# Linear attention and MLP-mixer on one core: the last batch's products pair by pair, its outputs on other queues, single load buffers from batch 4 on

## The chip, the cores and the metric

The kernel runs on one core of one Trainium2 chip. The metric is the device time of one execution in microseconds (us). The profile's span is some 1.8 us shorter than the device time (262.1 against 263.9 for the profiled run of before); it runs from the first instruction to the end of the last.

## The reference

```python
# q, k, v: [8 batches, 8 heads, 576, 64]
phi = lambda x: np.where(x > 0, x, np.exp(x) - 1.0) + 1.0
kv  = einsum('bhsd,bhse->bhde', phi(k), v);  z = phi(k).sum(axis=2)
x   = einsum('bhsd,bhde->bhse', phi(q), kv) / (einsum('bhsd,bhd->bhs', phi(q), z)[..., None] + 1e-6)
x   = x.transpose(0, 2, 1, 3).reshape(8, 576, 512)
u   = x + (relu(x.T @ w_tok1) @ w_tok2).T        # token mixing, per batch
out = u + relu(u @ w_ch1) @ w_ch2                # channel mixing, 512 -> 1536 -> 512
```

## The kernel before

Batches are taken one after the other. While TensorE (PE) does the channel mixing of batch n, the attention and token mixing of batch n + 1 and the preparation of batch n + 2 are put in between its matmuls at fixed steps. The order on every engine is the order of the program; no scheduler changes it.

576 rows are four row tiles of 128 and a rest of 64. The rests ("tails") of two batches share one tile, which is done with the odd batch. In batches 6 and 7 the last matrix product of the four row tiles is not done tile by tile. Two row tiles (pair j, 0 or 1) and two halves of the columns make a 2 by 2 block matrix, which is multiplied with seven products in place of eight (Strassen's scheme). Each product is six matmuls of 256 columns. Products 1, 6, 7 and 4 add up in one PSUM tile, X (where the matmuls leave their sums), which VectorE (DVE) must read between them:

```python
def product(n, j, i):          # i: which of the seven, j: which pair of row tiles
    lhs, rhs, tile_, first = {1: (..., "X", True),  2: (..., "Z", True), 6: (..., "X", False),
                              5: (..., "Y", True),  7: (..., "X", False), 4: (..., "X", False),
                              3: (..., "Y", False)}[i]
    ...                        # six matmuls into the PSUM tile, then DVE adds it to o
    if i in (4, 3):            # a row tile is complete: two transfers of 128 KB
        d, r = (1 if i == 4 else 0), 2 * j + (1 if i == 4 else 0)
        for e in range(2):
            nc.gpsimd.dma_start(out=outv[n, :, 2 * r + e], in_=o[half[e], d])

ORDER = [(1, 0), (1, 1), (2, 0), (6, 0), (2, 1), (6, 1), (5, 0), (7, 0), (5, 1), (7, 1),
         (4, 0), (3, 0), (4, 1), (3, 1)]
```

The very last work is the shared tail tile, in a part of 384 and one of 128 columns, whose outputs go out on SP's and ScalarE's (ACT's) queues:

```python
def mm4_last(cs):
    ...                        # 12 matmuls, one DVE addition
    for b in range(2):
        (nc.scalar if b else nc.sync).dma_start(out=outv[2 * p + b, :, 2 * R, cs], in_=o[half[b]])
...
big = m3(n) + m3t + m4s(n) + [                                   # batch 7
    lambda: mm4_last(slice(0, DM - 128)), lambda: mm4_last(slice(DM - 128, DM))]
```

Operands that the seven products need are sums of weight blocks (GpSimd, once) and of activation blocks ("row sums", DVE, in each of the two batches). They are kept in load buffers that are no longer used.

## Time and profile before

| | before |
|---|---|
| device time, median of 3 runs (263.83 with the fourth, which the comparison below has) | 263.8 us (263.64 to 263.93) |
| span of the profile | 262.1 us |
| PE busy | 249.9 us |
| start of PE's last matmul | 254.97 us |
| from there to the end of the span | 7.16 us |

The chain of waits that ended last, in order of time; the columns are start in us, us, and what. These are its last pieces:

```profile
249.30 0.67 PE h_ps L605 x6
...
251.50 0.45 POOL out_dram L629
...
254.09 1.04 POOL out_dram L629 x2
255.13 0.52 POOLq L895
```

The reader is to see that the chain leaves PE at 249.97 and runs to the end through GpSimd (POOL): through its eight output issues and then through "POOLq L895", GpSimd's sequencer at the kernel's closing line. It says that GpSimd stood at the end of what the program waited for last. The chain stops at 255.65 although the span ends at 262.1, so it doesn't say what GpSimd did in the rest.

### The profile page before, as it was taken

How to read it: one execution, taken by the hardware profiler on the slowest of the kernel's cores; microseconds unless marked ns; L12 is line 12 of the kernel's file. 1: busy time of each engine (PE TensorE's matmuls, PEld its weight loads, DVE VectorE, ACT ScalarE, POOL GpSimd, SP SyncE). 2: the span in 40 equal slices, each digit the busy share in tenths (PEclk: the TensorE clock that was granted, in tenths of full speed). 3: DMA queues.
4: the chain of work that ended last, by engine and by line, in shares of the span. 5: the costliest groups of instructions: out<-in, count | busy, mean ns of one | idle time of the engine just before them, and what ended most of it. 6: DMA issues, size and time to landing. Idle time of an engine off the chain costs nothing.

```text
span 262.1 us, 5249 instructions
## 1 busy us (share of the span) xinstructions
PE 249.9 (95%) x2142; PEld 138.4 (53%) x2142; DVE 161.9 (62%) x317; ACT 131.2 (50%) x205; POOL 65.6 (25%) x92
## 2 busy tenths in 40 slices
PE   7799999999999999999999999999999999999990
PEld 3574465646644544455644544455644545756970
DVE  5875859865966376837652575838862486815550
ACT  4755853387580569146670569046670543046100
POOL 9850300110011100110003100179909500060060
PEclk9999999999999999999999999999999999999996
DMA  7999999799049951899999972660083403350033
GB/s 254 254 204 293 351 232 399 243 265 407 9 114 198 393 210 25 179 258 406 409 253 172 373 277 42 149 164 0 16 156 81 123 0 23 80 160 3 0 100 103
DMA packets 49576, 48.35 MB, mean 184 GB/s; under 512 B 30288, under 2 KB 35536, under 8 KB 49552
## 3 DMA queue, kind: packets, MB, share of 16 engines
q1 hardware_dynamic: 41184, 34.35, 43.6%
q0 software_dynamic: 8208, 13.54, 23.3%
q8 instruction: 17, 0.28, 0.5%
q10 hardware_dynamic: 160, 0.13, 0.2%
q14 instruction: 7, 0.06, 0.1%
HBM read 35.85 MB, written 9.44 MB: 173 GB/s over the span
## 4 chain that ended last, share of the span: by engine, by line
PE 79%; DMA 10%; POOL 3%; DVE 2%; issue 1%; ACT 1%; POOLq 0%; DVEq 0%
PE c_ps L480 28%; PE h_ps L506 26%; DMA wc<-in_moe_w_ch_dram 7%; PE a_ps L246 6%; PE c_ps L494 4%; PE h_ps L259 4%; PE nd_ps L208 3%; PE h_ps L605 3%; DMA cr<-in_v_dram 3%; PE kv_ps L167 2%; PE y_ps L605 1%; POOL out_dram L629 1%; DVE o_sb L611 1%; POOL qT L673 1%; DVE ut L284 1%
## 5 line engine op out<-in xcount | busy, mean ns | idle before, releaser
L487 ACT ACTIVATE cr<-c_ps 128x512 bf16<-128x512 f32 x91 | 53.5, 599 | 77.2 <-PE c_ps L480 77.1
L480 PE MATMUL c_ps<-uT,wc 128*128 128x512 bf16 x384 | 91.4, 379 | 0.1
L506 PE MATMUL h_ps<-wc,cr 128*128 128x512 bf16 x288 | 66.0, 379 | 0.4 <-DMA wc<-in_moe_w_ch_dram 0.4
L480 PEld LDWEIGHTS <-wc 128*128 128x128 bf16 x384 | 35.7, 98 | 36.7 <-issue 1.7
L528 POOL DMA_DIRECT2D out_dram<-o_sb x24 | 14.5, 608 | 130.8 <-DVE o_sb L523 130.6
L506 PEld LDWEIGHTS <-cr 128*128 128x128 bf16 x288 | 27.4, 98 | 32.2 <-DMA wc<-in_moe_w_ch_dram 0.9
L220 DVE TENSOR_TENSOR x<-nd_ps,den 128x512 bf16<-128x512 f32 (+1 forms) x42 | 25.3, 602 | 1.5
L523 DVE TENSOR_TENSOR o_sb<-h_ps,u 128x512 f32<-128x512 f32 x24 | 16.4, 689 | 13.2 <-PE h_ps L506 13.0
L124 ACT ACTIVATE e<-q_raw 128x1152 bf16<-128x1152 f32 x16 | 18.5, 1160 | 5.6 <-DMA q_raw<-in_q_dram 5.4
L138 DVE TENSOR_TENSOR qp<-e,y 128x1152 bf16<-128x1152 bf16 x16 | 12.3, 770 | 12.3 <-ACT e L124 11.8
L124 ACT ACTIVATE e<-k_raw 128x1152 bf16<-128x1152 f32 x16 | 18.7, 1169 | 2.4 <-DMA k_raw<-in_k_dram 2.4
L217 DVE TENSOR_SCALAR den<-nd_ps 128x8 f32<-128x8 f32 (+1 forms) x42 | 6.9, 163 | 19.9 <-PE nd_ps L208 19.2
L271 DVE TENSOR_TENSOR u<-h_ps,x 128x1024 bf16<-128x1024 f32 x12 | 14.7, 1222 | 6.2 <-PE h_ps L259 6.2
L629 POOL DMA_DIRECT2D out_dram<-o_sb x16 | 8.3, 527 | 40.4 <-DVE o_sb L611 40.4
L138 DVE TENSOR_TENSOR kp<-e,y 128x1152 bf16<-128x1152 bf16 x16 | 12.1, 757 | 8.0 <-ACT e L124 7.4
L208 PEld LDWEIGHTS <-qT 128*128 128x128 bf16 x140 | 11.4, 98 | 9.3 <-issue 0.2
L208 PE MATMUL nd_ps<-kvbd,qT 128*128 128x130 bf16 x140 | 15.1, 223 | 0.0
L246 PE MATMUL a_ps<-x,w 128*128 128x512 bf16 x56 | 14.4, 379 | 0.0
L130 DVE TENSOR_SCALAR y<-q_raw 128x1152 bf16<-128x1152 f32 x16 | 13.6, 849 | 0.9 <-DMA q_raw<-in_q_dram 0.9
L149 ACT CAST vs<-v_raw 128x1152 bf16<-128x1152 f32 x12 | 13.9, 1160 | 0.0
L130 DVE TENSOR_SCALAR y<-k_raw 128x1152 bf16<-128x1152 f32 x16 | 12.0, 753 | 1.4 <-DMA k_raw<-in_k_dram 1.3
L259 PE MATMUL h_ps<-ar,w2p 128*128 128x512 bf16 x48 | 12.3, 379 | 0.0
(120 smaller groups left out, 282.9 us busy)
## 6 DMA issues: line engine op xcount, KB each, us to landing
k_raw<-in_k_dram SPq DMA_DIRECT2D x16, 576.0 KB, 9.8
q_raw<-in_q_dram SPq DMA_DIRECT2D x16, 576.0 KB, 7.1
v_raw<-in_v_dram SPq DMA_DIRECT2D x14, 576.0 KB, 11.1
out_dram<-o_sb POOLq DMA_DIRECT2D x24, 256.0 KB, 5.0
wc<-in_moe_w_ch_dram POOLq DMA_DIRECT2D x8, 384.0 KB, 9.3
out_dram<-o_sb POOLq DMA_DIRECT2D x22, 128.0 KB, 3.4
cr<-in_v_dram POOLq DMA_DIRECT2D x2, 288.0 KB, 6.9
w<-in_moe_w_tok_dram POOLq DMA_DIRECT2D x1, 288.0 KB, 7.2
```

What stands on the lines that cost most here:

```text
L124: nc.scalar.activation(out=e, in_=f, func=AF.Exp)
L130: nc.vector.tensor_scalar(out=y, in0=f, scalar1=1.0, scalar2=1.0, op0=ALU.add, op1=ALU.max)
L138: nc.vector.tensor_tensor(out=dst.transpose([0, 2, 1, 3]), in0=e.rearrange("p (i t d) -> p i t d", i=nj, t=T), in1=y.rearrange("p (i t d) ...
L208: nc.tensor.matmul(out=o[:, a], lhsT=qT[b][:, t0:t0 + 128], rhs=kvbd[b][:, c, a], start=True, stop=True)
L220: nc.vector.tensor_tensor(out=x[b][:, rs[0]:rs[0] + m, HG * D * g:HG * D * (g + 1)].rearrange("p r (h d) -> p r h d", h=HG), in0=v_[:, :, ...
L246: nc.tensor.matmul(out=ps[:, mt], lhsT=w1t[:, b, ms] if r == R else w1[:, r, ms], rhs=x[b][:, r, :], start=(r == 0), stop=(r == R))
L259: nc.tensor.matmul(out=ps[:, i], lhsT=w2v(kt, r, b), rhs=ar[b][:, kt, :], start=(kt == 0), stop=(kt == NT - 1 and not add))
L271: nc.vector.tensor_tensor(out=u[b][:, rs[0]:rs[0] + m], in0=ps[:, 0:m], in1=x[b][:, rs[0]:rs[0] + m], op=ALU.add)
L480: nc.tensor.matmul(out=ps, lhsT=wc1[:, kj, 128 * mc:128 * mc + 128], rhs=uT[b][:, :, kj], start=(kj == 0), stop=(kj == NDM - 1))
L487: nc.scalar.activation(out=cr[b][:, mc, :], in_=ps, func=AF.Relu)
L506: nc.tensor.matmul(out=ps, lhsT=crt[:, kc, :] if t == 8 else cr[b][:, kc, 128 * r:128 * r + 128], rhs=wc2[:, kc, :], start=(kc == 0), stop ...
L523: nc.vector.tensor_tensor(out=o, in0=ps, in1=u[b][:, r, :], op=ALU.add)
```

## The change

Its intent: the last batch's first pair of row tiles is completed, and sent out, long before the end; GpSimd issues none of the last batch's outputs; the tail tile fills a wait between two products. From batch 4 on each tensor has one load buffer instead of two, with loads about one batch ahead, which frees buffers so that the weight sums can start early in batch 5. The tails' token mixing is moved behind batch 6's products. (The diff is cut; where the operands' buffers are renamed it only follows from this.)

```diff
+    def rb(n):
+        return n % 2 if n < 4 else 0
-        return after(nc.sync.dma_start(out=raw[nm, n % 2][:, js], in_=src_[:, js]), gate)
+        return after(nc.sync.dma_start(out=raw[nm, rb(n)][:, js], in_=src_[:, js]), gate)
 ...
-    def mm4_last(cs):            # (removed)
 ...
-        if i in (4, 3):
-            d, r = (1 if i == 4 else 0), 2 * j + (1 if i == 4 else 0)
+        queues = [nc.sync, nc.scalar] if n + 1 == B else [nc.gpsimd] * 2
+        if n + 1 == B and j == 1 and i in (2, 4, 3):
+            d, cs = {2: (0, HC[0]), 4: (1, ALL), 3: (0, HC[1])}[i]
             for e in range(2):
-                nc.gpsimd.dma_start(out=outv[n, :, 2 * r + e], in_=o[half[e], d])
+                queues[e].dma_start(out=outv[n, :, 2 * (2 * j + d) + e, cs], in_=o[half[e], d, cs])
+        elif i == 3:
+            for e in range(2):
+                queues[e].dma_start(out=outv[n, :, 4 * j + e:4 * j + e + 3:2], in_=o[half[e]])
 ...
+    LAST = [(1, 0), (2, 0), (6, 0), (5, 0), (7, 0), (1, 1), (4, 0), (3, 0),
+            (2, 1), (6, 1), (5, 1), (7, 1), None, (4, 1), (3, 1)]     # None: the tail tile
 ...
-                big = m3(n) + m3t + m4s(n) + [
-                    lambda: mm4_last(slice(0, DM - 128)), lambda: mm4_last(slice(DM - 128, DM))]
+            big = m3(n) + m3t + (m4(p, [4, 5, 6, 7, 8]) if n < FIRST else
+                                 m4s(n) + m4(p, [8]) if n + 1 < B else m4s(n, LAST))
 ...
+            if n >= FIRST:
+                at_.update(mm2t=25, utt=25)
 ...
-            fill += [(18, lambda: load_all(n + 4, "qkv"))]
-        if n + 3 == B:
-            fill += [(18 + i, lambda i=i: weight_sums(2 * i, 2)) for i in range(3)]
+            fill += [(k_[1] + 2, lambda: load_all(n + 3, "qkv"))]
+        if n + 1 == FIRST:
+            fill += [(4 * i, lambda i=i: weight_sums(2 * i, 2)) for i in range(3)]
```

More of the change, by code (lines that the diff above doesn't have):

```diff
@@ L121, in phi_exp @@
     def phi_exp(nm, n, j0, nj):
-        f = raw[nm, n % 2][:, j0:j0 + nj].rearrange("p j f -> p (j f)")
+        f = raw[nm, rb(n)][:, j0:j0 + nj].rearrange("p j f -> p (j f)")
         e = work.tile([128, 2 * TD], BF16, name="e", tag="e", bufs=4)[:, :nj * TD]
@@ L127, in phi_add @@
     def phi_add(nm, n, j0, nj):
-        f = raw[nm, n % 2][:, j0:j0 + nj].rearrange("p j f -> p (j f)")
+        f = raw[nm, rb(n)][:, j0:j0 + nj].rearrange("p j f -> p (j f)")
         y = work.tile([128, 2 * TD], BF16, name="y", tag="y")[:, :nj * TD]
@@ L149, in vcast @@
         copy(out=vs[:, js, :, 0:D],
-             in_=raw["v", n % 2][:, js].rearrange("p j (t d) -> p j t d", t=T))
+             in_=raw["v", rb(n)][:, js].rearrange("p j (t d) -> p j t d", t=T))
     def bank():
@@ L535, in mm4_end @@
                 put.dma_start(out=outv[2 * p + b, :, 2 * R], in_=o[half[b]])
-    def mm4_last(cs):
-        p = B // 2 - 1
-        m = cs.stop - cs.start
-        ps = ps_big.tile([128, 512], FP32, name="h2_ps", tag="big")[:, 0:m]
-        for kc in range(NCH):
-            nc.tensor.matmul(out=ps, lhsT=crt[:, kc, :],
-                             rhs=wc2[:, kc, cs], start=(kc == 0), stop=(kc == NCH - 1))
-        o = outp.tile([128, 2, DM], FP32, name="o_sb", tag="o_sb")[:, 0, 0:m]
-        nc.vector.tensor_tensor(out=o, in0=ps, in1=ut[p % 2][:, cs], op=ALU.add)
-        for b in range(2):
-            (nc.scalar if b else nc.sync).dma_start(out=outv[2 * p + b, :, 2 * R, cs],
-                                                    in_=o[half[b]])
     KH = NCH // 2
@@ L557, in bf @@
         return t[:, 1536 * i:1536 * (i + 1)]
-    tb = [bf("k", 0, i).rearrange("p (k c) -> p k c", k=KH) for i in range(3)] + [
-        bf("q", 0, 0).rearrange("p (k c) -> p k c", k=KH)]
-    tf = raw["q", 0].rearrange("p j f -> p (j f)")[:, 768:2304].rearrange("p (k c) -> p k c", k=KH)
-    sb = [(bf("v", 0, i) if i < 3 else bf("v", 1, 0)).rearrange("p (k j s) -> p k j s", k=KH, j=2)
+    FIRST = 6
+    tb = [bf("k", 1, i).rearrange("p (k c) -> p k c", k=KH) for i in range(3)] + [
+        bf("q", 1, 0).rearrange("p (k c) -> p k c", k=KH)]
+    tf = raw["q", 1].rearrange("p j f -> p (j f)")[:, 768:2304].rearrange("p (k c) -> p k c", k=KH)
+    sb = [(bf("v", 1, i) if i < 3 else bf("q", 1, 1)).rearrange("p (k j s) -> p k j s", k=KH, j=2)
           for i in range(4)]
@@ L625, in product, with m4s @@
             add(0, 1, ps, o[:, 0, HC[1]])
-        if i in (4, 3):
-            d, r = (1 if i == 4 else 0), 2 * j + (1 if i == 4 else 0)
+        queues = [nc.sync, nc.scalar] if n + 1 == B else [nc.gpsimd] * 2
+        if n + 1 == B and j == 1 and i in (2, 4, 3):
+            d, cs = {2: (0, HC[0]), 4: (1, ALL), 3: (0, HC[1])}[i]
             for e in range(2):
-                nc.gpsimd.dma_start(out=outv[n, :, 2 * r + e], in_=o[half[e], d])
+                queues[e].dma_start(out=outv[n, :, 2 * (2 * j + d) + e, cs], in_=o[half[e], d, cs])
+        elif i == 3:
+            for e in range(2):
+                queues[e].dma_start(out=outv[n, :, 4 * j + e:4 * j + e + 3:2], in_=o[half[e]])
     ORDER = [(1, 0), (1, 1), (2, 0), (6, 0), (2, 1), (6, 1), (5, 0), (7, 0), (5, 1), (7, 1),
              (4, 0), (3, 0), (4, 1), (3, 1)]
-    def m4s(n):
-        return [lambda i=i, j=j: product(n, j, i) for i, j in ORDER]
+    LAST = [(1, 0), (2, 0), (6, 0), (5, 0), (7, 0), (1, 1), (4, 0), (3, 0),
+            (2, 1), (6, 1), (5, 1), (7, 1), None, (4, 1), (3, 1)]
+    def m4s(n, order=ORDER):
+        out_ = []
+        for e in order:
+            out_ += [lambda e=e: product(n, e[1], e[0])] if e else m4(n // 2, [8])
+        return out_
     def prep_k(n, g, copy=nc.scalar.copy):
@@ L846 @@
         if b == 0:
-            big = m3(n) + (m4s(n) if n + 2 == B else m4(p, [0, 1, 2, 3]))
+            big = m3(n) + (m4s(n) if n >= FIRST else m4(p, [0, 1, 2, 3]))
         else:
-            big = m3(n) + m3t + m4(p, [4, 5, 6, 7, 8])
-            if n + 1 == B:
-                big = m3(n) + m3t + m4s(n) + [
-                    lambda: mm4_last(slice(0, DM - 128)), lambda: mm4_last(slice(DM - 128, DM))]
+            big = m3(n) + m3t + (m4(p, [4, 5, 6, 7, 8]) if n < FIRST else
+                                 m4s(n) + m4(p, [8]) if n + 1 < B else m4s(n, LAST))
         fill = []
         if n + 1 < B:
-            fill += [((AT3 if n == 2 else AT)[nm], fn) for nm, fn in steps(n + 1)]
+            at_ = dict(AT3 if n == 2 else AT)
+            if n >= FIRST:
+                at_.update(mm2t=25, utt=25)
+            fill += [(at_[nm], fn) for nm, fn in steps(n + 1)]
         if n + 2 < B:
@@ L859 @@
             fill += [(12 + d, lambda: qtr_dma(n + 2))]
-            if n == 2:
-                fill += [(16, lambda: load_all(5, "qkv"))]
-            fill += [(s + d, lambda g=g: prep_k(n + 2, g)) for g, s in ((0, 14), (1, 16))]
-            fill += [(18, lambda: load_all(n + 4, "qkv"))]
-        if n + 3 == B:
-            fill += [(18 + i, lambda i=i: weight_sums(2 * i, 2)) for i in range(3)]
-        if n + 2 >= B:
+            k_ = ((14, 16) if n < FIRST else (18, 20) if b == 0 else (14, 21))
+            fill += [(s + d, lambda g=g: prep_k(n + 2, g)) for g, s in enumerate(k_)]
+            fill += [(k_[1] + 2, lambda: load_all(n + 3, "qkv"))]
+        if n + 1 == FIRST:
+            fill += [(4 * i, lambda i=i: weight_sums(2 * i, 2)) for i in range(3)]
+        if n >= FIRST:
             fill += [(9, lambda n=n: row_sums(n, 3, 0, KH))]
```

## The prediction

> **What bounds the kernel now.** I read the page first, then PE's own waits, then the timeline of the last two batches, then the transfers. The page:
>
> ```profile
> PE 249.9 (95%) x2142; PEld 138.4 (53%) x2142; DVE 161.9 (62%) x317; ACT 131.2 (50%) x205; POOL 65.6 (25%) x92
> ...
> PE   7799999999999999999999999999999999999990
> ```
>
> PE (TensorE) is busy in every slice but the first and the last. What PE waits for is therefore the whole budget between them. These are the longest:
>
> ```profile
> PE bank L653 <- DVE ones L666: 1.5, 1, 1.5
> PE bank L178 <- DVE qp L138: 1.3, 1, 1.3
> PE h_ps L605 <- DVE o_sb L611: 0.5, 1, 0.5
> ```
>
> The first two lie in the first 9 us, which the change doesn't touch. No load from batch 1 on makes PE wait. The third lies in batch 6's products (L605: the seven-product scheme that stands in for the last matrix product in batches 6 and 7). Its timeline, cut to that stretch:
>
> ```profile
> 221.47 0.62 PE L280 MATMUL h_ps<-ar,w2p 128*64 128x512 bf16 x4
> 222.03 1.08 PE L605 MATMUL h_ps<-k_raw,v_raw 128*128 128x256 bf16 x6
> ...
> 224.26 0.82 PE L605 MATMUL y_ps<-k_raw,v_raw 128*128 128x256 bf16 x6
> 225.62 0.82 PE L605 MATMUL h_ps<-k_raw,v_raw 128*128 128x256 bf16 x6 [0.54 <-DVE o_sb L611]
> ```
>
> Products start 0.655 us apart when nothing is late (226.27, 226.93, 227.58). So 222.03 to 222.95 holds 0.27 us of waiting (for a row sum that DVE ends at 222.56), and 224.26 to 225.62 holds 0.70: DVE spent 223.73 to 225.11 on the tail's two additions (L284, 0.69 each) and read the accumulator of product 6 only afterwards. The end of the run:
>
> ```profile
> 251.50 4.15 POOL L629 DMA_DIRECT2D out_dram<-o_sb  x8 [18.06 <-DVE o_sb L611]
> ...
> 252.41 2.78 PE L543 MATMUL h_ps<-wc,crt 128*128 128x384 bf16 x24
> ...
> 254.56 0.96 DVE L546 TENSOR_TENSOR o_sb<-h_ps,ut 128x384 f32<-128x384 f32 x2 [1.52 <-PE h_ps L543]
> 255.15 1.19 SPq L548 DMA_DIRECT2D out_dram<-o_sb  x2
> 255.15 1.46 ACTq L548 DMA_DIRECT2D out_dram<-o_sb  x2
> ```
>
> PE issues its last matmul at about 255.03 (call the end of issue T; the row adds 0.16 us of modelled drain, the difference between a 0.82 row and its 0.655 spacing). GpSimd takes 4.15 us to issue eight 128 KB outputs, the last at 255.13. SP and ACT issue four small ones, the last on ACT at about 255.83, landing 3.8 us later by the transfer view: 259.6, or T + 4.6. From there to 262.1 is a close of about 2.5 us.
>
> **What the Trainium skill says.** "DMA: Bandwidth & Descriptors", section "Issuing engines are not separate DMA queues": transfers from all engines run on the same 16 DMA engines, and issuing from several saves only issue time. The trace agrees: DMA is still moving some 240 GB/s from 253 to 258 whoever issued it. The same page, "Anatomy of one DMA", puts most of a transfer's roughly 2 us fixed cost into the write receipt; here outputs of 32 to 128 KB take 2.9 to 4.1 us from issue to landing, little of it size. "SBUF — State Buffer", in its terms, calls the port pair that VectorE and GpSimd share an exclusive lock for a whole instruction. The trace agrees for the q addition that runs beside GpSimd's subtractions: 1.72 us against 0.75 alone, while the subtraction takes 1.67 against 1.16.
>
> **The change part by part.**
>
> *Buffers.* Loads for batches 5, 6 and 7 go to one set of buffers, about a batch before use rather than nearly two. Before, twelve loads were issued from 110.2 to 124.7 and six from 139.5 to 145.9. Now six go after each of three batches' preparation. Batch 5's q is still issued near 110.2 (the SP queue reaches it after the transpose there) and first read at 122.64. Batch 7's follow the tails' transpose, 166.95 + 1.41 = 168.4, and are first read by DVE at 181.16. The median q landing between 130 and 165, with crowded queues, was 6.7 us. Both have 12 us. k and v follow later and have their readers from 131.8 and 189.8. Effect on PE: 0.
>
> *Weight sums.* 18 GpSimd subtractions at 1.16 us start after the same output issues near 173.7 and run through, to about 195 to 197, where six of them ran from 197.85 to 204.6 before. They now overlap batch 7's k additions on DVE (189.8 and 192.8, 0.75 us each, to become perhaps 1.7). DVE was idle 1.90 us waiting for PE soon after, and four PSUM banks of 2.6 us work each stand between its output additions and PE. Effect: 0.
>
> *Tail of batches 6 and 7 moved behind batch 6's last product.* DVE loses 1.38 us in the critical stretch, so the second wait (0.70) goes. But L280 leaves the place where it filled time: product 6 would start at 221.38, run three matmuls (0.33) to 221.71, then wait for the row sum until 222.61. That is 0.90 of waiting in place of 0.27, and the four matmuls (some 0.56) are run later. Sum of the waits: 0.99 + 0.09 of switching before, 0.90 + 0.09 after, so -0.1 us. The transposes after it start near 232; their reader starts at 240.5.
>
> *Last batch's order.* Products of one row pair now follow each other: 1, 2, 6, 5, 7. Product 6 may overwrite nothing before DVE has read product 1, and only one product (0.655) lies between. DVE starts 0.20 after the product's issue ends and takes 0.425, and PE restarts 0.055 after DVE (225.565 to 225.62 above): 0.68 against 0.655, 0.03 us lost. It happens at four places (1 to 6, 6 to 7, 7 to 4, and 6 to 7 of the second pair): +0.1 us. Before, two products lay between.
>
> *Tail tile undivided.* 12 matmuls of 512 columns in place of 12 of 384 and 12 of 128: the same columns; twelve of 512 show 2.75 at 200.59 against 2.78. 0.0.
>
> *Outputs.* The first pair's 512 KB leave at T - 5.9 and are out of the way. GpSimd's eight issues vanish for this batch. But DVE now does the tail (0.69) at T - 1.11, product 4 to T, and product 3 from T + 0.20 to T + 0.62. SP, at 0.55 us an issue plus 0.05 between, has two for the tail from T - 0.37, one for product 4 at T + 0.83 and the last at T + 1.43; ACT starts its last at T + 0.7. Last issue T + 1.43 against T + 0.80 before, 0.63 later. About 640 KB is written in those last microseconds, less than the 1.25 MB of before, so I estimate 3.3 us to landing rather than 3.8, chosen between the 2.9 and 3.8 seen: T + 4.7 against T + 4.6, +0.1 us.
>
> Sum: 0 + 0 - 0.1 + 0.1 + 0.0 + 0.1 = +0.1, so 263.8 becomes 263.9 us.
>
> **Rivals.** First: the end is shorter than I think. For it: GpSimd was issuing until 255.65, and if its queue holds the close open, or if SP and ACT land in 2.9 us without its traffic, 0.3 to 0.6 us are gained: 263.3. Against: the last landing by my reckoning was ACT's, not GpSimd's. Second: SP's row of three issues and the burst behind it give 3.8 us to landing or more, and PE's four restarts lose 0.1 to 0.2 rather than 0.03: +0.6 to +0.9, 264.5. For it: SP really is in order. Third: a load comes too late in its single buffer, as its issue now waits for the previous batch's casts: PE would stand for a microsecond or more, 265. Against: the 12 us of lead. Fourth: GpSimd's lock delays DVE so that PE misses a PSUM bank, up to 1 us, against which stand the four banks.
>
> **Range and chances.** All terms are tenths of microseconds in a span that PE fills; 2% would be 5.3 us, ten times any of them. The spread of the runs of before is 0.3 us. Rival one gives the lower end and rival two the upper: 263.2 to 264.6. Chances: faster by over 2% 0.01, within 2% 0.97, slower by over 2% 0.02.
>
> **What would show it.** Batch 6: no wait of PE on DVE's output addition between products 5 and 7, a wait near 0.9 us inside product 6, and L280's successor behind the last product. Batch 7: four gaps of 0.03 us. Batches 3 to 5: no wait of DVE or ACT on a load. DVE's k addition near 190 longer than 1 us. End: two tail issues before SP's last two, the last SP issue 1.4 us after T, nothing from GpSimd. I would be wrong if ACT or DVE waits on a load of batches 5 to 7, if the close after the last landing isn't 2.5 us, or if batch 6's stretch from 218.55 to 230.20 (11.65 us) isn't 11.5 to 11.6 after.

## The result, and the profile after

The changed kernel took 262.0 us (median of four runs, 261.91 to 262.42) against 263.83 of before (263.64 to 263.93). The ratio is 0.9935, with a 95% interval of 0.9918 to 0.9952. Ratios here are the mean time of one kernel's runs over that of the other's of the same rounds, so not quite the ratio of the medians. The forecast that the time stays within 2% held, but 262.0 lies 1.2 us below the range, and the predicted sign was wrong.

PE's waits of the kernel after, longest first (total us, times, longest); only the third concerns the change:

```profile
PE bank L653 <- DVE ones L666: 1.5, 1, 1.5
PE bank L181 <- DVE qp L141: 1.2, 1, 1.2
PE h_ps L595 <- DVE v_raw L577: 0.7, 1, 0.7
```

Batch 6's products in the timeline of after (start, us, engine, line, operation, shapes, count; in brackets the idle time before, and what ended it):

```profile
221.31 0.49 PE L595 MATMUL h_ps<-k_raw,v_raw 128*128 128x256 bf16 x3
...
222.54 0.50 PE L595 MATMUL h_ps<-k_raw,v_raw 128*128 128x256 bf16 x3 [0.74 <-DVE v_raw L577]
...
224.84 0.82 PE L595 MATMUL h_ps<-k_raw,v_raw 128*128 128x256 bf16 x6
...
229.52 0.62 PE L283 MATMUL h_ps<-ar,w2p 128*64 128x512 bf16 x4
```

The wait before product 7 is gone (224.84 follows 224.19 by one product), product 6 now stands still in its middle, and the tails' four matmuls are at the end. That is what the prediction drew. Now the end of the run, from the timeline of after, with the same columns:

```profile
253.66 0.82 PE L595 MATMUL h_ps<-q_raw,cr 128*128 128x256 bf16 x6
254.31 0.82 PE L595 MATMUL y_ps<-wc,q_raw 128*128 128x256 bf16 x6
254.58 1.11 SPq L538 DMA_DIRECT2D out_dram<-o_sb  x2
255.17 0.42 DVE L601 TENSOR_TENSOR o_sb<-y_ps,o_sb 128x256 f32<-128x256 f32 x1 [0.23 <-PE y_ps L595]
255.78 1.37 SPq L620 DMA_DIRECT2D out_dram<-o_sb  x2
```

PE's last matmul starts at 254.86, 0.11 earlier than before, and SP's row of issues ends at 257.15, later than the 256.34 of before. Yet the span ends at 260.2 instead of 262.1. So the gain is not on PE. The table divides each span by the first of batch n's channel-mixing matmuls (us):

| stretch | before | after |
|---|---|---|
| start, batches 0 and 1 (to the first of batch 2) | 84.93 | 84.85 |
| batch 2 | 27.25 | 27.26 |
| batch 3 | 31.87 | 31.87 |
| batch 4 | 27.25 | 27.26 |
| batch 5 | 31.87 | 31.87 |
| batch 6 | 27.02 | 26.97 |
| batch 7, to the start of the last matmul | 24.77 | 24.78 |
| last matmul to the end of the span | 7.16 | 5.32 |

Of 1.96 us, 1.84 are in the last line. The windows view of that stretch has the columns window, length, busy time of five engines, granted clock, DMA share and GB/s. Before:

```profile
258.50:259.00 0.50, 0.00 (x0) 0.00 (x0) 0.00 (x0) 0.00 (x0) 0.00 (x0) 0.50 0.23 69
259.00:259.50 0.50, 0.00 (x0) 0.00 (x0) 0.00 (x0) 0.00 (x0) 0.00 (x0) 0.50 0.00 0
```

After:

```profile
258.00:258.50 0.50, 0.00 (x0) 0.00 (x0) 0.00 (x0) 0.00 (x0) 0.00 (x0) 0.61 0.88 312
258.50:259.00 0.50, 0.00 (x0) 0.00 (x0) 0.00 (x0) 0.00 (x0) 0.00 (x0) 0.50 0.00 0
```

The last byte moves less than half a microsecond earlier; what follows the last byte shrinks from over 3 us to under 2. The page and the timeline leave out what sequencers do, so I read their records in the trace. A DRAIN is an instruction of an engine's sequencer; these stand at the kernel's closing line (L895), ahead of a closing barrier, at which every engine has to have arrived before the program goes on. These are the rows that decide, put in my words (start us, us, engine, operation; first before, then after):

```
before  254.77  6.58  POOL  DRAIN              until 261.35
        259.62  0.03  SP    wait for the last transfer to land (ACT's, landed 259.61)
        260.00  0.01  SP    arrives at the closing barrier
        261.39  0.02  POOL  finds all arrived, releases the barrier

after   230.77  7.35  POOL  DRAIN              until 238.12
        258.96  0.03  SP    wait for the last transfer to land (SP's, landed 258.94)
        259.40  0.01  SP    arrives at the closing barrier
        259.43  0.02  POOL  finds all arrived, releases the barrier
```

Before, everything had landed and SP was at the barrier at 260.00, but GpSimd, which releases the barrier, was inside a DRAIN until 261.35. After, its DRAIN was over at 238.12, and the barrier followed SP by 0.03. With the same 0.03, the barrier of before would have been at 260.03, so the DRAIN cost 1.36 us. ACT shows no such thing: its DRAIN in before ended at 257.06, 2.55 us before its own last transfer landed, and it is SP that waits, one semaphore after another, for the transfers of all queues.

The other 0.60 of the 1.96 are SP's earlier arrival: 0.11 from PE, 0.56 because the last landing comes 4.08 us after the last matmul's start rather than 4.64, less 0.07 because SP's chain of waits after it is that much longer. The chain view of after no longer has GpSimd at its end; this is its last piece:

```profile
255.17 0.42 DVE o_sb L601
```

### The profile page after: what moved, and what is told of

The parts are those of the page before. It is cut to its first block, busy times and chain, and to the rows that moved or that the text cites. A ratio compares the mean times of both kernels' runs of the same rounds, so it can differ in the third digit from the quotient of the medians.

```text
span 260.2 us, 5195 instructions
## 1 busy us (share of the span) xinstructions
PE 249.1 (96%) x2113; PEld 137.7 (53%) x2130; DVE 164.1 (63%) x316; ACT 130.8 (50%) x205; POOL 61.9 (24%) x80
## 4 chain that ended last, share of the span: by engine, by line
PE 81%; DMA 8%; ACT 3%; POOL 3%; DVE 2%; issue 1%; SPq 0%; POOLq 0%; DVEq 0%; ACTq 0%
PE c_ps L483 28%; PE h_ps L509 26%; PE a_ps L249 5%; PE h_ps L595 4%; PE c_ps L497 4%; DMA k_raw<-in_k_dram 4%; DMA wc<-in_moe_w_ch_dram 4%; PE h_ps L262 4%; PE nd_ps L211 3%; PE y_ps L595 2%; PE kv_ps L170 2%; ACT e L127 1%; POOL qT L673 1%; POOL cr L119 1%; PE h_ps L283 1%
## 5 line engine op out<-in xcount | busy, mean ns | idle before, releaser
L531 POOL DMA_DIRECT2D out_dram<-o_sb x24 | 14.5, 608 | 125.0 <-DVE o_sb L526 124.8
L141 DVE TENSOR_TENSOR kp<-e,y 128x1152 bf16<-128x1152 bf16 x16 | 12.9, 805 | 6.7 <-ACT e L127 6.0
L133 DVE TENSOR_SCALAR y<-k_raw 128x1152 bf16<-128x1152 f32 x16 | 13.7, 856 | 2.9 <-DMA k_raw<-in_k_dram 2.8
L497 PE MATMUL c_ps<-uTt,wc 128*128 128x128 bf16 x192 | 12.0, 219 | 0.0
```

The lines of the kernel that those rows point to most:

```text
L133: nc.vector.tensor_scalar(out=y, in0=f, scalar1=1.0, scalar2=1.0, op0=ALU.add, op1=ALU.max)
L141: nc.vector.tensor_tensor(out=dst.transpose([0, 2, 1, 3]), in0=e.rearrange("p (i t d) -> p i t d", i=nj, t=T), in1=y.rearrange("p (i t d) ...
L497: nc.tensor.matmul(out=ps[:, m], lhsT=wc1[:, kj, 128 * mc:128 * mc + 128], rhs=uTt[:, kj, :], start=(kj == 0), stop=(kj == NDM - 1))
```

## The experiments

Theory D: GpSimd's DRAIN at the close lasts until some 2 us after GpSimd's own last transfer has landed (form 1), or 6.6 to 7.4 us from its own start as in the two traces (form 2), and it held the end. Theory O: the gain comes from the new order of the last batch (the first pair out early, fewer bytes at the end). Theory B: it comes from the buffers, weight sums or tails. All twelve runs gave the correct result. Four calls were made, each on one chip with its own runs of before (medians 263.87, 263.8, 264.01 and 263.88).

### The queues alone

`e1_before_hw_queues` is the kernel before with this edit:

```diff
-                nc.gpsimd.dma_start(out=outv[n, :, 2 * r + e], in_=o[half[e], d])
+                put = nc.gpsimd if n + 1 < B else nc.scalar if e else nc.sync
+                put.dma_start(out=outv[n, :, 2 * r + e], in_=o[half[e], d])
```

> The kernel before, with one edit: the sixteen... that is eight output transfers of batch 7's products that GpSimd issued go half to SP's and half to ACT's queue; order, tails and buffers stay as before. Theory D (GpSimd's closing drain, which ended 2.5 us after the last landing of GpSimd's own transfers, held the end of the program for 1.36 us, and the GpSimd traffic delayed the others' landings): the drain ends early, the last landing comes near 258.5 to 258.9, and the time is 261.6 to 262.1, nearly the whole gain of the change. Theory O (the gain is the order of the last batch: first pair out early, fewer bytes at the end): nothing or a few tenths, 263.4 to 263.9. Theory B (buffers or tails): 263.8.

Measured: 261.43 us (ratio 0.9909, 0.9896 to 0.9922). The DRAIN ended at 237.99, and from the last matmul to the end it took 4.69 us. The time lies 0.17 below what theory D expected. The queues alone bring the whole gain, and a little more than the change. Theory B falls, and O as the main cause.

### The queues undone

`e2_after_gpsimd` is the changed kernel with `queues = [nc.gpsimd] * 2` for every batch.

> The changed kernel with one part undone: batch 7's product outputs go back to GpSimd, in the new order and grouping; the tails' tile stays on SP. Theory D: GpSimd's last issue starts near 256.6, lands about 3 us later, the drain ends 2.0 to 2.5 us after that and the time is 263.8 to 264.8, above even the kernel before, since the new order gives GpSimd its last pieces later. Theory O: near 262.0, at most 262.6. Theory B: 262.0.

Measured: 264.62 us (1.0029, 1.0017 to 1.0041), 0.3% slower than before. GpSimd's last transfer landed at 259.23, its DRAIN lasted until 262.08 (2.85 later, where 2.0 to 2.5 were expected), and the barrier was released at 262.12 although SP was there at 259.70. The new order without the new queues is a loss, as GpSimd then has its last pieces later.

### One transfer on GpSimd

`e3_one_gpsimd` is the changed kernel with one half of the last product's output on GpSimd:

```diff
-                queues[e].dma_start(out=outv[n, :, 2 * (2 * j + d) + e, cs], in_=o[half[e], d, cs])
+                put = nc.gpsimd if i == 3 and e else queues[e]
+                put.dma_start(out=outv[n, :, 2 * (2 * j + d) + e, cs], in_=o[half[e], d, cs])
```

> The changed kernel with a single 64 KB transfer, half of the very last product's output, moved from ACT to GpSimd. Theory D, form 1 (the drain ends 2.0 to 2.5 us after the last landing of GpSimd's transfers): the transfer is issued near 255.65, lands near 258.5, the drain ends near 260.7 and the time is 263.0 to 263.6. Theory D, form 2 (the drain lasts 6.6 to 7.4 us from its own start, as in both traces): drain from about 255.7 to 262.6, time 264.9 to 265.3. Theories O and B: 262.0.

Measured: 263.44 us (0.9993, 0.9976 to 1.001): a single 64 KB transfer gives back most of the gain. The timeline of this run, GpSimd alone:

```profile
257.29 0.54 POOL L621 DMA_DIRECT2D out_dram<-o_sb  x1 [24.34 <-DVE o_sb L601]
```

(The profiled execution was one of the slower ones of this kernel, 264.63, and everything in it from batch 1 on stands 1.4 us later.) The transfer landed at 259.99 and the DRAIN ran from 257.27 to 262.08, 4.81 us. So the DRAIN has no fixed length, and form 2 falls. It ended 2.09 after the landing, as form 1 has it, and the barrier was released 1.19 after SP's arrival.

### Early transfers on GpSimd

`e4_early_gpsimd` is the changed kernel with `nc.gpsimd` for the first pair's two transfers.

> The changed kernel with only the first row pair's outputs of batch 7 (512 KB in two transfers, issued near 249.1) on GpSimd, six microseconds before the end. Theory D, form 1: they land by about 254 and the drain is over by 256.5, before the other queues' landings, so 262.0 (within 0.2). A theory that any GpSimd traffic in the last batch costs the close its 1.4 us: 263.4.

Measured: 262.19 us (0.9942, 0.9927 to 0.9956), the same as the changed kernel. GpSimd landed at 254.10 and its DRAIN was over at 256.23, before SP reached the barrier at 259.53. GpSimd's traffic in the last batch shows no cost by itself; a late end of it does.

The DRAINs of these traces together (us from each span's start):

| kernel | GpSimd's last landing | DRAIN | its end after the landing | SP at the barrier | barrier released |
|---|---|---|---|---|---|
| before | 258.81 | 254.77 to 261.35 | 2.54 | 260.00 | 261.39 |
| after | 236.07 | 230.77 to 238.12 | 2.05 | 259.40 | 259.43 |
| e1_before_hw_queues | 235.78 | 232.68 to 237.99 | 2.21 | 259.02 | 259.05 |
| e2_after_gpsimd | 259.23 | 256.64 to 262.08 | 2.85 | 259.70 | 262.12 |
| e3_one_gpsimd | 259.99 | 257.27 to 262.08 | 2.09 | 260.93 | 262.12 |
| e4_early_gpsimd | 254.10 | 249.83 to 256.23 | 2.13 | 259.53 | 259.56 |

### The buffers undone

`e5_buffers_back` is the changed kernel with two load buffers to the end:

```diff
     def rb(n):
-        return n % 2 if n < 4 else 0
+        return n % 2
-            fill += [(k_[1] + 2, lambda: load_all(n + 3, "qkv"))]
+            if n == 2:
+                fill += [(16, lambda: load_all(5, "qkv"))]
+            fill += [(18, lambda: load_all(n + 4, "qkv"))]
-            fill += [(4 * i, lambda i=i: weight_sums(2 * i, 2)) for i in range(3)]
+            fill += [(18 + i, lambda i=i: weight_sums(2 * i, 2)) for i in range(3)]
```

(and the operands' buffers as before).

> The changed kernel with its buffer part undone: two load buffers per tensor to the end, loads two batches ahead, weight sums late in batch 5 as before. Theory D (drain of GpSimd at the end) and the prediction's own zero for this part: 262.0, within 0.3. Theory B (the loads' spread over the batches gives part of the gain): 262.5 to 263.

Measured: 261.69 us (0.9918, 0.9904 to 0.9931), 0.01 below what was expected. Batches 2 to 5 take 27.25, 31.87, 27.26 and 31.87 us: to 0.01 what they take in both other kernels. The single buffers cost and gain nothing where they act. The third of a microsecond against the changed kernel's first measurement doesn't stand there: in the profiles 0.21 of the spans' 0.25 lie before batch 2 (84.64 against 84.85), and in the repeat on another chip (below) the changed kernel took 261.80.

### The tails undone

`e6_tails_back` is the changed kernel with `at_.update(mm2t=14, utt=14)`.

> The changed kernel with the tails' tile of batches 6 and 7 back between batch 6's products. By the prediction's sum this part is worth 0.1 us, so 262.1 (261.9 to 262.4), with a PE wait of about 0.5 us on DVE before product 7 back in batch 6. If the tails held more than that, 262.6 or more.

Measured: 262.48 us (0.9946, 0.9932 to 0.996), 0.08 above what was expected. Batch 6 takes 27.09 us against 26.97, the predicted 0.1. The wait is back:

```profile
226.28 0.81 PE L595 MATMUL h_ps<-k_raw,v_raw 128*128 128x256 bf16 x6 [0.61 <-DVE o_sb L601]
```

The rest of the difference between the two profiles stands before batch 2, where the program is the same: batch 1 took 32.92 us there and 32.24 in the changed kernel. Why these builds differ in their first two stages stays open; among all profiles, batch 1 took from 32.23 to 32.92. So the timed runs alone don't show the 0.1; batch 6's stretch does.

### Attempts at a better end

`e7_tail_two_queues` is the changed kernel with the tail tile's second half on ACT, so that SP has one issue less in its row:

```diff
-                put.dma_start(out=outv[2 * p + b, :, 2 * R], in_=o[half[b]])
+                (nc.scalar if last and b else put).dma_start(out=outv[2 * p + b, :, 2 * R], in_=o[half[b]])
```

> The changed kernel with the second half of the tail tile's output on ACT's queue in place of SP's, so that each queue has three issues at the end. With the drain gone the last landing of SP's row sets the end: the last issue moves from 256.5 to about 255.9 and the time falls by 0.4 to 0.6, to 261.4 to 261.6. If bytes in flight rather than issue set the last landing: 261.9 to 262.0.

Measured: 261.79 us (0.9923, 0.9909 to 0.9937). SP's last issue moved to 0.92 us after the last matmul's start from 1.64, but ACT, now with the tail's half in its row, had its last at 1.20. The end shrank from 5.32 to 5.10: half of what was expected, and not distinct from the changed kernel in the timed runs.

`e8_both` is `e7_tail_two_queues` with a product of batch 6 moved as well, `ORDER = [(1, 0), (1, 1), (2, 0), (2, 1), (6, 0), (6, 1), ...]`.

> As the run before, and batch 6's second pair's product 2 goes ahead of the first pair's product 6, whose row sums are 0.74 us late. PE's wait there falls from 0.74 to about 0.2 us: 260.8 to 261.1, below both kernels. If another wait takes its place: as the run before.

Measured: 261.74 us (0.9922, 0.991 to 0.9935), nothing gained, where 260.8 to 261.1 had been hoped for. Another wait took the place, in the timeline of this run:

```profile
222.32 1.07 PE L595 MATMUL h_ps<-k_raw,v_raw 128*128 128x256 bf16 x6
223.88 0.81 PE L595 MATMUL h_ps<-k_raw,v_raw 128*128 128x256 bf16 x6 [0.49 <-DVE o_sb L601]
```

Product 6 of the first pair still holds 0.25 us of waiting (1.07 against 0.82), and that of the second pair starts 1.56 us after it rather than 0.655, so 0.25 + 0.65 = 0.90, as much as the 0.90 that one product held in the changed kernel (222.54 less 221.31 less three matmuls, 0.33). Batch 6 takes 26.96 us against 26.97. The likely reason is that DVE works down one row of additions and row sums there, so that PE's order only chooses where to wait for it; that is not shown, as no run shortens DVE's row.

`after_again` is the changed kernel once more.

> The changed kernel once more, unaltered, as the measure for the other two of this call: 262.0 (261.8 to 262.3).

Measured: 261.80 us (261.77 to 262.11; 0.9919, 0.9904 to 0.9934).

`e9_order_back` is the changed kernel with batch 7's order, 128 KB pieces and divided tail tile of before, on SP and ACT.

> The changed kernel with batch 7's order, pieces and divided tail tile of before, but all of its outputs on SP and ACT. If the new order was worth something beside the queues, it is slower than the changed kernel. By run e1 (before with the queues alone: 4.69 us from PE's last matmul to the end, against 5.32 in the changed kernel) it should be 0.5 to 0.7 faster: 261.3 to 261.5.

Measured on the same chip as `after_again`: 261.44 us (0.9904, 0.9888 to 0.992), and 4.76 us from the last matmul to the end. With the queues moved, what the change does to batch 7's order, pieces and tail tile costs about 0.4 us (this run undoes the three together). The likely reason is that its end has larger last pieces, in a row on SP. The transfer view (size, median us from issue to landing) of `e1_before_hw_queues`, which ends in the same way as this run:

```profile
out_dram<-o_sb SPq DMA_DIRECT2D x1, 32.0 KB, 2.2
out_dram<-o_sb ACTq DMA_DIRECT2D x1, 32.0 KB, 2.1
```

and of the changed kernel, for the window of SP's last issue:

```profile
out_dram<-o_sb SPq DMA_DIRECT2D x1, 64.0 KB, 2.4
```

`e10_tail_last` keeps the new order of pairs, but does the tail tile last, in its two parts of before.

> The changed kernel with its order of pairs and its queues, but the tails' tile last again and in two parts, 384 and 128 columns, so that the last transfers are of 32 KB, with nothing queued ahead of them. If the row of issues and the size of the last pieces set what is left of the end, PE's last matmul to the end falls from 5.32 to about 3.9 to 4.2 and the time is 260.6 to 261.0, below both kernels. If the end is bound by the bytes in flight: 261.4.

Measured: 261.60 us (0.9917, 0.9898 to 0.9937), 0.6 above what was hoped for. The end fell to 4.15 us as expected, but batch 7 grew from 24.78 to 25.55:

```profile
251.50 0.81 PE L611 MATMUL h_ps<-q_raw,cr 128*128 128x256 bf16 x6 [0.52 <-DVE o_sb L617]
```

This is the second pair's product 4, right behind its product 7, waiting for DVE to read X. In the change the tail tile stands exactly there. I had taken away what filled the wait.

`e11_gap_filled` puts the second pair's product 2 there (the edit against `e10_tail_last`):

```diff
-            (2, 1), (6, 1), (5, 1), (7, 1), (4, 1), (3, 1)]
+            (6, 1), (5, 1), (7, 1), (2, 1), (4, 1), (3, 1)]
```

> As e10, where product 4 of the second pair followed its product 7 at once and batch 7 took 25.55 us from its first matmul to its last in place of 24.78; here that pair's product 2 stands between them. If that adjacency is the 0.77 us, batch 7 is back at 24.8 to 24.9, the end stays at 4.1 to 4.3 us after PE's last matmul and the time is 260.6 to 261.0, below both kernels and below e9's 261.44. If the product moved late costs its own transfer on the queues, the end grows to 4.6 and the time is 261.2.

Measured: 261.1 us, median of six from 260.78 to 261.85 (0.9896, 0.9877 to 0.9916). That is 0.1 above what was hoped for. Batch 7 is back at 24.88 and the end is 4.15, as expected. It is faster than before. Its ratio is below both of the changed kernel's (0.9935 and 0.9919), but its interval overlaps that of the repeat (0.9904 to 0.9934), and its six runs spread over 1.07 us, so that lead is likely and not shown. Its lead over `e9_order_back` (0.9904) is within the spread.

## Why the prediction was wrong, point by point

**Buffers, 0 us: right.** The trace of after shows no wait of DVE or ACT on a load after the first 60 us, and the stages agree to 0.01. `e5_buffers_back` shows the same from the other side.

**Weight sums, 0 us: right, and with the side effect foreseen.** DVE's two additions for batch 7's k took 1.43 and 1.72 us beside GpSimd in place of 0.75, and PE didn't notice.

**Tails, -0.1 us: right in kind, half in size.** Batch 6 went from 27.02 to 26.97; `e6_tails_back` gives 0.12. The new wait is where it was drawn (0.90 expected, 0.90 measured).

**The order, +0.1 us, and the undivided tile, 0.0: right within 0.1.** Product 6 starts at 244.46 where 244.44 would have been without a wait, 0.02 rather than 0.03, and batch 7 changes by 0.01 altogether. (The end point of that stretch is the start of the last matmul, which is a 256-column one after and a 128-column one before, so a few hundredths are not comparable.)

**Outputs, +0.1 us: wrong, and this is the whole miss.** The stretch went from 7.16 to 5.32, so it was -1.84. Two terms in it failed.

The first and larger is the sentence "From there to 262.1 is a close of about 2.5 us", which took the close of before for a constant. It is not: it was 2.5 because GpSimd's DRAIN was still running, and is 1.2 after (260.17 less 258.94). The DRAIN was worth 1.36 us. "If the close after the last landing isn't 2.5 us" was one of the prediction's own signs of being wrong, and it came true. The prediction named the cause as its first rival ("if its queue holds the close open"), and put it aside with "the last landing by my reckoning was ACT's, not GpSimd's". The landing was ACT's indeed (259.61 against GpSimd's 258.81). But the argument assumed that what lands last ends last. In the traces GpSimd's DRAIN goes on for 2.05 to 2.85 us after its last landing, while SP arrives at the barrier 0.39 to 0.46 us after the last landing of all in the two kernels, so the earlier landing gave the later end. The chain view, which ended in "POOLq L895", spoke for the rival; the prediction doesn't use it.

The second is "I estimate 3.3 us to landing rather than 3.8". With T for the end of issue of PE's last matmul, as there, the last issue did come late: 1.53 us after T (256.50) against 0.80 in before, 0.73 later where 0.63 was expected. But its 64 KB landed in 2.44 us, so the last landing was 0.56 earlier from the last matmul rather than 0.1 later. That the landing was quicker because GpSimd's megabyte was no longer moving beside it agrees with the 3.6 and 3.8 us for 32 KB of before against 2.2 and 2.1 in `e1_before_hw_queues`, where that same megabyte was issued on SP and ACT, in 2.8 us (251.35 to 254.13) in place of 4.15. How much of it is contention and how much the kind of queue was not separated; in `e3_one_gpsimd` the 64 KB took 2.70 us from issue to landing on GpSimd, against 2.78 for the same piece on ACT in the changed kernel, so for that one the kind of queue made little difference.

The rivals' sizes: the first was put at 263.3, half a microsecond of gain; the close was held open and the landing was quicker, as it says, and it was more than three times too small (1.8 us measured). The second, third and fourth did not come.

**Slips in the working that changed nothing.** The two waits of batch 6 are 0.27 and 0.70, which is 0.97 and not 0.99. The DMA traffic of before from 253 to 258 is 218 GB/s on the mean, not 240, and doesn't by itself show that the issuing engine is of no account. The section "Anatomy of one DMA" of the Trainium skill's "DMA: Bandwidth & Descriptors" is about transfers that GpSimd issues, and was applied to SP's and ACT's as well; that most of the fixed cost is the write receipt is not shown here: the last landing came 0.68 us after the last packet's end in before and 0.39 in after.

## What to carry to other kernels

An output transfer can have a cost after its landing, and here it differed from engine to engine. A single 64 KB transfer issued by GpSimd at the end cost about 1.4 us that the same transfer on ACT did not (263.44 against 262.0, or 1.6 against the repeat's 261.80), so let the last outputs go out on SP and ACT, and keep GpSimd for earlier ones. Small last pieces seem to help: with nothing late on GpSimd, the runs that ended with 32 KB pieces took 4.15 to 4.76 us from the last matmul to the end, those with 64 KB 5.10 to 5.39. When a term of a sum is called a constant, ask what ends it: follow the chain of waits to its last entry, and if that is an engine whose work was done long before, look at what its sequencer is doing. And a piece of work that looks movable may be standing in a gap on purpose (`e10_tail_last`).

## What the Trainium skill lacked or had wrong

- "VectorE: DVE Perf Modes", section "The DRAIN you can't avoid", knows two kinds of DRAIN: one after each VectorE operation, and boilerplate around a kernel of some 12 ns, constant, on all five engines. The DRAINs that stand at this kernel's closing line fit that for SP (0.01 us), but the first ones of the others there took, in before and after, 1.84 and 2.80 us on PE, 0.33 and 0.46 on DVE, 0.41 and 0.40 on ACT. GpSimd's took 6.58 and 7.35 us in the two kernels, from 4.81 to 7.35 in all six traces of the table, and held the end of the program where GpSimd had issued late transfers.
- No page has how GpSimd's closing DRAIN depends on its transfers: it ended 2.05 to 2.85 us after the landing of GpSimd's last one, in six traces.
- "DMA: Bandwidth & Descriptors", section "Issuing engines are not separate DMA queues", says that issuing from several engines only saves the sequencer's time to issue. For eight transfers at the end of the program, moving them from GpSimd to SP and ACT alone took 263.87 to 261.43 us. Of these 2.44 us, 1.36 are the DRAIN's cost in the trace of before, which is no time of issue; the rest was not divided into issue, contention and kind of queue.
